# A fused Fourier-mixing and attention kernel: an earlier wait on the last value product, row steps and casts moved between engines, zero rows loaded from DRAM

## The chip, the cores and the metric

The kernel runs on one core of a Trainium2 chip. A core has a matrix engine (TensorE; in the profile PE for its matmuls and PEld for its weight loads), a vector engine (VectorE, DVE), a scalar engine (ScalarE, ACT), a general engine (GpSimd, POOL), and a sync engine (SP) that here issues most DMA transfers. Each engine works through its own list of instructions in order; semaphores make one wait for another. The metric is the device time of one execution, in microseconds (us).

## The reference

Inputs are a sequence x of 2048 rows and 512 columns, two pairs of DFT matrices (2048x2048 and 512x512, real and imaginary), the weights of an attention layer with 32 heads of 16 columns, and a gate vector.

```python
x = A_x
g = sigmoid((x * gate_w).sum(-1, keepdims=True))
a = x @ dft_hid_re.T ;  b = x @ dft_hid_im.T
fourier = dft_seq_re @ a - dft_seq_im @ b
q, k, v = split(x @ wqkv)                     # 32 heads, 16 columns each
p = softmax(q @ k.T * 16 ** -0.5)             # per head, 2048 x 2048
attention = concat(p @ v) @ wo
out = g * fourier + (1 - g) * attention
```

All is in 32-bit floats. The weights of the attention layer are drawn large, so the scores are large, and the maximum of each row has to be subtracted before the exponential.

## The kernel before

**Split operands.** Most matmuls take operands in a fast 32-bit format that keeps fewer bits. A number is therefore split into a rounded part and a rest (a cast and a subtraction, `hi_lo` at line 101 and similar pairs of lines), and a product is the sum of three matmuls.

**Pairs of heads.** The 32 heads are taken as 16 pairs p. For each pair two tiles, `qs` and `ks` (two buffers each, so pairs p and p + 2 share one), hold on 128 partitions two stacks of 64 rows, one for each head h of the pair. Rows 0 to 47 of a stack are the split parts of q and k. Rows 48 and 49 of `ks` are ones, and the same rows of `qs` hold the negated row maximum, again in two parts, so that the score matmul subtracts the maximum by itself. Rows 50 to 63 are zeros. `load_stacks` (line 264) loads a pair's stacks on SP's queue; the ones and zeros are put in at the start (lines 327 to 335), from a small tile that has the tile name `hl` in the profile, and from the third pair on `load_stacks` clears the two maximum rows from a DRAM tensor of zeros, `z_d`.

**Row maxima ahead of scores.** Each score tile (128x512) is computed twice. `a_tile` (line 281) multiplies q by k for a tile and VectorE reduces it to row maxima (`mx`, line 289). When 64 such tiles, half a pair (p, hf), are done, two row steps are put into the list `deferred`. `m_parts` (line 296) takes the maximum over the four tiles of a row, negated (`nm`), and splits it into `nhl`. `m_rows` (line 304) transposes `nhl` into `mt` on VectorE and issues eight DMAs that write it as rows 48 and 49 of `qs`, some on SP's queue, the others on GpSimd's. Later `scores` (line 772) computes the transposed tile with these rows and ScalarE takes its exponential into `pt` (line 786).

**Value products.** A unit u is one block of 128 keys for one half of the queries of a pair; its four exponential tiles lie in `pts[u]`. `pv` (line 813) multiplies them by v, in four column strips of the array at a time, into the accumulator bank `acc` (line 829). A 32-bit matmul runs here as two instructions, so that a unit has eight in the profile. `evacuate` (line 799) copies `acc` on ScalarE (line 806) and GpSimd adds the copy to a running total (line 807). After two segments of half a pair the total is stored.

**Fourier matmuls beside it.** The DFT chains (`real`, `dft`, then `proj` for the output projection; matmuls at line 461) are cut into half-height matmuls of 64 rows. Each runs on one half of the array while a score or maxima matmul, which has 64 rows too, runs on the other. Chunks of the DFT matrices are loaded on SP's queue (`craw`), and `c_split` (line 437) splits them on GpSimd (lines 445 and 446).

**The order is written out by hand.** `segment` (line 936) goes through a pattern of slots. A slot with a letter issues one Fourier matmul and, beside it, a maxima tile (a) or a score tile (s); a digit names its PSUM bank; a bar issues the value products of one unit. There are short phases THIN and NINE at the ends, and in between 192 segments with this pattern:

```python
FULL = "a5 s4 a2 s0 a3 s6 a5 s4 s1 s0 s2 a6 a3 a4 s5 a1 | |"
```

The accumulator shares bank 6 with a6, and it is closed and copied out at each segment's end. The last value product of a FULL segment has an added wait on the last exponential issued (line 951), which is that of s5, in slot 14. At the end of a segment one entry of `deferred` is run, so that `m_parts` stands at the end of one segment and `m_rows` at the end of the next. In the FULL phase the 64th tile of a half pair comes at slot 6.

**Blocks.** Finished heads are normalised in 12 blocks (`block`, line 602): step 0 loads, step 1 multiplies on GpSimd, step 2 splits the result and stores it; here the cast is on ScalarE (line 102) and the subtraction on GpSimd (line 103). `run_plan` runs such steps at fixed units, ahead of a segment.

Of the kernel before, what the change touches and what calls it, by code (L numbers as in the profile page):

```python
# [17 lines left out]
D = 512  # L18
# [13 lines left out]
def mix_kernel(ctx: ExitStack, tc: tile.TileContext, xa_t, xa, wqkv, w_hid, w_seq, wo, gate_w, out):  # L32
# [40 lines left out]


    qk_d = [dram.tile([2, D, S], F32, name=f"qk{c}") for c in range(2)]
    z_d = dram.tile([2, S], F32, name="z")
    b_d = [dram.tile([P, 2, D], F32, name=f"b{s}") for s in range(NT)]
    o_d = [dram.tile([NP, 64, S // 2], F32, name=f"o{hf}") for hf in range(2)]
    yr_d = [dram.tile([P, D], F32, name=f"yr{t}") for t in range(NT)]
# [184 lines left out]
    def load_stacks(p):  # L264
        q_t, k_t = qs[p % 2], ks[p % 2]
        for h in range(2):
            rows = slice((2 * p + h) * DH, (2 * p + h + 1) * DH)
            o = 64 * h
            if p > 1:
                nc.sync.dma_start(q_t[o + 48:o + 50].bitcast(F32), z_d)  # L270

            for i, (qv, kv) in enumerate(((0, 0), (0, 1), (1, 0))):
                part = slice(o + 16 * i, o + 16 * i + 16)
                nc.sync.dma_start(q_t[part].bitcast(F32), qk_d[0][qv, rows])
                nc.sync.dma_start(k_t[part].bitcast(F32), qk_d[1][kv, rows])
# [5 lines left out]
    def a_tile(i, h, ps=None, bank=None):  # L281
        p, j = divmod(i, 64)
        qt, kb = divmod(j, 4)
        if ps is None:
            ps = psA.tile([P, 512], F32, "a", bank)
        r = slice(64 * h, 64 * h + 64)
        nc.tensor.matmul(ps, qs[p % 2][r, qt * P:(qt + 1) * P], ks[p % 2][r, kb * 512:(kb + 1) * 512],  # L287
                         start=True, stop=True)
        user = nc.vector.tensor_reduce(mx[p % 2][:, h, qt, kb:kb + 1], ps, AX.X, ALU.max)  # L289
        hf = j // 32  # L290
        a_left[p, hf] = a_left.get((p, hf), 64) - 1
        if not a_left[p, hf]:
            deferred.extend((partial(m_parts, p, hf), partial(m_rows, p, hf)))
        return user

    def m_parts(p, hf):

        nc.vector.tensor_reduce(nm[hf].rearrange("p (q h) -> p h q", h=2), mx[p % 2][:, :, 8 * hf:8 * hf + 8, :],
                                AX.X, ALU.max, negate=True)
        t = nhl[hf]  # L300
        nc.gpsimd.tensor_copy(t[:, 0], nm[hf])
        nc.gpsimd.tensor_tensor(t[:, 1], nm[hf], t[:, 0].bitcast(F32), ALU.subtract)

    def m_rows(p, hf):

# [21 lines left out]
    for i in range(2):  # L327
        for h in range(2):
            for tb in range(2):
                cols = slice(tb * 2 * D, (tb + 1) * 2 * D)  # L330
                nc.sync.dma_start(ks[i][64 * h + 48:64 * h + 50, cols].bitcast(F32), ones)
                nc.sync.dma_start(ks[i][64 * h + 50:64 * h + 64, cols].bitcast(F32), zeros[:14])
                nc.sync.dma_start(qs[i][64 * h + 48:64 * h + 64, cols].bitcast(F32), zeros)
    for tb in range(2):
        nc.sync.dma_start(z_d[:, tb * 2 * D:(tb + 1) * 2 * D], zeros[:2])
    wrs = []
    a_next = 0

# [263 lines left out]
    def block(step, hf, ct, half):  # L602

        if step == 0:
            t = work.tile([P, 2, D], F32, name="no")
            load_o(t[:, 0], t[:, 1], hf, ct, half * D)
            blocks[hf, ct] = t
        elif step == 1:
            t = blocks[hf, ct]
            nc.gpsimd.tensor_tensor(t[:, 0], t[:, 0], t[:, 1], ALU.mult)  # L610
        else:
            t = blocks.pop((hf, ct))
            hl = work.tile([P, 2, D], F32R, name="nh")
            hi_lo(hl[:, 0], hl[:, 1], t[:, 0], nc.gpsimd)
            nc.sync.dma_start(oh_d[hf][ct][:, :, half * D:(half + 1) * D], hl.bitcast(F32))

    last_o = []
# [154 lines left out]
    def scores(u, qb, h, bank=(psS, "s"), number=None):  # L772
        p, r = divmod(u, 32)
        hf, kt = divmod(r, 16)
        q0 = hf * 1024 + qb * 512
        if u >= UNITS - 16:

            blk, kt = divmod(kt, 8)
            q0, kt = 1024 + blk * 512, 2 * kt + qb
        if u not in pts:  # L780
            pts[u] = work.tile([P, 4, 512], F32, name="pt", bufs=4)
        pool, name = bank
        ps = pool.tile([P, 512], F32, name=name) if number is None else pool.tile([P, 512], F32, name, number)
        rr = slice(64 * h, 64 * h + 64)
        nc.tensor.matmul(ps, ks[p % 2][rr, kt * P:(kt + 1) * P], qs[p % 2][rr, q0:q0 + 512], start=True, stop=True)  # L785
        return nc.scalar.activation(pts[u][:, 2 * qb + h], ps, AF.Exp, bias=0.0, scale=DH ** -0.5)  # L786

# [22 lines left out]
                nc.sync.dma_start(o_d[hf][p, :, qb * 512:(qb + 1) * 512], total[64 * qb:64 * qb + 64])  # L810
            total = None

    def pv(u, full=False, close=False):
        nonlocal acc
        if u >= UNITS - 16:
            return pv_last(u)
        p, r = divmod(u, 32)
        hf, kt = divmod(r, 16)
        pt = pts.pop(u)
        begin, done = acc is None or kt == 0, kt == NT - 1  # L820
        if acc is None:
            acc = psO.tile([P, 512], F32, "acc")
            if not full:
                nc.vector.memset(acc, 0.0)  # L824
        width = 32 if full and begin else 17
        v = vt[:, kt].rearrange("p n d -> p (n d)")[:, 33 * p:]
        for j in range(4):
            h = j % 2
            i = nc.tensor.matmul(acc[32 * j:32 * j + width], v[:, 16 * h:16 * h + width], pt[:, j],  # L829
                                 start=begin, stop=done or close)  # L830
# [86 lines left out]
    thin = 1 + 4 * (NT - 3)  # L917
    streams = [stream(h) for h in range(2)]

    users, valued, exponential = [], 0, None  # L920

    def score(kind, h, number=None):
        nonlocal exponential
        x = next(streams[h][kind == "a"], None)
        if x:
            users.append((kind, a_tile(*x, bank=number) if kind == "a" else scores(*x, number=number)))
            if kind == "s":
                exponential = users[-1][1]

    def values(full=False, close=False):  # L930
        nonlocal valued
        i = pv(valued, full, close)
        valued += 1
        return i

    def segment(pattern, half, ds, stop):
# [4 lines left out]
        ds, turned = iter(ds), False  # L941
        for n, slot in enumerate(pattern.split()):
            number = None
            if slot[1:].isdigit():
                slot, number = slot[0], int(slot[1])
            if slot == "|":
                end = n == len(pattern.split()) - 1
                i = values(pattern == FULL, end and (pattern == FULL or valued == thin))
                if end and pattern == FULL:

                    tc.add_manual_dep(i.ins, exponential.ins.name,
                                      mybir.DependencyInfo(mybir.DependencyClass.Sync, mybir.DependencyReason.DATA))
                while between:
                    between.pop(0)()
# [123 lines left out]
```

## Time and profile before

| | us |
|---|---|
| three runs | 1697.93, 1702.73, 1703.36 |
| their median | 1702.73 |
| the profiled execution, device time | 1700.88 |
| its span, first to last instruction | 1699.1 |
| TensorE busy in the span | 1683.4 |
| VectorE busy | 1371.5 |
| ScalarE busy | 1250.0 |
| GpSimd busy | 661.6 |
| mean granted TensorE clock | 0.997 |

How to read it: the page and the views give times from the span's start. A group row has line, engine, operation, tiles (out<-in), shapes, count, then busy us and mean ns of one, then the idle time of the engine ahead of the group and what ended most of it. A row of waits is: who waited, for what, us in total, times, the longest. A row of the timeline is: start, duration, engine, line, operation, with neighbours of one group merged and their count after x. TensorE's busy time overlaps its own pipelining, so 99% does not say that nothing can be gained there; the idle and the length of a stage say more.

### The profile page before, as it was taken

To read this page: it belongs to the slowest core of one execution; us is meant where nothing else is said; L and a number is where in the kernel's file an instruction comes from. 1 tells how busy PE (TensorE), PEld (TensorE's weight loads), DVE (VectorE), ACT (ScalarE), POOL (GpSimd) and SP (SyncE) were. 2 spreads that over 40 slices of the span, in tenths; PEclk is the share of its full clock that TensorE was granted. 3 is DMA by queue.
4 is the path that set the end of the run, shared out by engine and by line. 5 is a ranking of instruction groups with operands and counts; after the bars stand their busy time and mean duration, and the time that the engine had idled before them with its cause. 6 is when DMAs were issued, how large, how long until landed. Compare 5 with 4: busy or idle time off the path is not lost.

```text
span 1699.1 us, 34567 instructions
## 1 busy us (share of the span) xinstructions
PE 1683.4 (99%) x13040; PEld 1024.1 (60%) x13040; DVE 1371.5 (81%) x2290; ACT 1250.0 (74%) x2435; POOL 661.6 (39%) x724
## 2 busy tenths in 40 slices
PE   9999999999999999999999999999999999999998
PEld 7878855556665656666565555556656556645444
DVE  5429888888888888888888888888888788889954
ACT  5212377787887888788877788878888788878886
POOL 0202112333544556444444465554444555421110
PEclk9999999999999999999999999999999999999999
DMA  9963600314241433314157434324142535452114
GB/s 290 349 141 132 184 10 2 58 33 82 57 77 46 85 101 94 77 39 83 38 95 249 97 102 108 76 60 73 52 83 70 118 99 103 141 169 46 35 32 138
DMA packets 82882, 166.63 MB, mean 98 GB/s; under 512 B 19760, under 2 KB 20254, under 8 KB 78818
## 3 DMA queue, kind: packets, MB, share of 16 engines
q1 hardware_dynamic: 78474, 163.45, 38.0%
q8 instruction: 103, 1.69, 0.5%
q0 software_dynamic: 3808, 0.30, 0.2%
q14 instruction: 65, 0.53, 0.1%
q10 hardware_dynamic: 432, 0.66, 0.1%
HBM read 108.19 MB, written 54.53 MB: 96 GB/s over the span
## 4 chain that ended last, share of the span: by engine, by line
PE 95%; DMA 3%; POOL 1%; issue 0%; SPq 0%; DVE 0%; ACT 0%; DVEq 0%; POOLq 0%
PE acc L829 28%; PE d L461 25%; PE a L287 17%; PE s L785 15%; PE s L375 3%; PE d L375 1%; PE acc L793 1%; DMA ks<-qk 1%; PE a L108 1%; PE a L106 1%; PE s L108 1%; PE s L106 1%; PE a L107 1%; PE s L107 1%; DMA raw<-wo 1%; PE s L461 1%
## 5 line engine op out<-in xcount | busy, mean ns | idle before, releaser
L289 DVE TENSOR_REDUCE mx<-a 128x1 f32<-128x512 f32 x2026 | 1258.8, 684 | 220.3 <-PE a L287 186.7
L786 ACT ACTIVATE pt<-s 128x512 f32<-128x512 f32 x2006 | 1022.6, 623 | 78.2 <-PE s L785 60.2
L287 PE MATMUL a<-ks,qs 64*128 64x512 f32 x2026 | 729.8, 405 | 2.5 <-DMA qs<-hl 2.5
L785 PE MATMUL s<-qs,ks 64*128 64x512 f32 x2006 | 692.8, 402 | 3.7 <-ACT few L806 2.7
L461 PE MATMUL d<-xab,ch 64*128 64x512 f32 x2016 | 646.3, 395 | 0.0
L829 PE MATMUL acc<-pt,vt 128*17 128x512 f32 (+1 forms) x3968 | 502.1, 600 | 2.0 <-DVE acc L824 2.0
L287 PEld LDWEIGHTS a<-ks,qs 64*128 64x128 f32 x2026 | 367.5, 184 | 224.5 <-issue 165.5
L807 POOL TENSOR_TENSOR oe<-oe,few 128x512 f32<-128x512 f32 x169 | 218.4, 1293 | 489.8 <-ACT few L806 481.4
L785 PEld LDWEIGHTS s<-qs,ks 64*128 64x128 f32 x2006 | 363.1, 184 | 65.3 <-issue 18.4
L461 PE MATMUL d<-xab,cl 64*128 64x512 f32 x1008 | 398.3, 395 | 0.0
L461 PEld LDWEIGHTS d<-xab,ch 64*128 64x128 f32 x2016 | 365.5, 184 | 29.3
L806 ACT COPY few<-acc 128x512 f32<-128x512 f32 x169 | 99.1, 586 | 189.4 <-PE acc L829 178.2
L829 PEld LDWEIGHTS acc<-pt,vt 128*17 128x17 f32 (+1 forms) x3968 | 103.6, 101 | 217.6 <-issue 155.7
L461 PEld LDWEIGHTS d<-xab,cl 64*128 64x128 f32 x1008 | 185.6, 184 | 15.1
L446 POOL TENSOR_TENSOR cl<-craw,ch 128x512 fp32r<-128x512 f32 x126 | 162.0, 1286 | 10.2
L445 POOL CAST ch<-craw 128x512 fp32r<-128x512 f32 x126 | 77.2, 613 | 52.9 <-PE s L785 31.6
L461 PE MATMUL d<-wre,xab 64*128 64x512 f32 x336 | 90.4, 402 | 0.0
L461 PEld LDWEIGHTS d<-wre,xab 64*128 64x128 f32 x336 | 58.8, 184 | 38.7 <-issue 23.3
L312 POOL DMA_DIRECT2D qs<-mt x119 | 67.0, 568 | 27.2 <-DVE mx L289 10.0
L461 PE MATMUL d<-wo_hl,o_hl 64*128 64x512 f32 (+1 forms) x246 | 68.1, 409 | 0.0
L461 PEld LDWEIGHTS d<-wo_hl,o_hl 64*128 64x128 f32 (+1 forms) x246 | 42.3, 184 | 29.8 <-issue 12.2
L102 ACT CAST hl<-s 128x512 fp32r<-128x512 f32 x28 | 16.1, 588 | 58.3 <-PE s L375 23.6
(171 smaller groups left out, 1044.1 us busy)
## 6 DMA issues: line engine op xcount, KB each, us to landing
craw<-w_seq SPq DMA_DIRECT2D x128, 256.0 KB
qk<-hl SPq DMA_DIRECT2D x32, 512.0 KB
qs<-qk SPq DMA_DIRECT2D x96, 128.0 KB
ks<-qk SPq DMA_DIRECT2D x96, 128.0 KB
b<-hl SPq DMA_DIRECT2D x16, 512.0 KB
xab<-b SPq DMA_DIRECT2D x16, 512.0 KB
o<-oe SPq DMA_DIRECT2D x62, 128.0 KB
oh<-nh SPq DMA_DIRECT2D x12, 512.0 KB
```

What stands on the lines that cost most here:

```text
L287: nc.tensor.matmul(ps, qs[p % 2][r, qt * P:(qt + 1) * P], ks[p % 2][r, kb * 512:(kb + 1) * 512], start=True, stop=True)
L289: user = nc.vector.tensor_reduce(mx[p % 2][:, h, qt, kb:kb + 1], ps, AX.X, ALU.max)
L312: (nc.gpsimd if own else nc.sync).dma_start(rows.rearrange("v (q b c) -> v b q c", q=8, b=4)[:, b], mt[hf][32 * b + h:32 * b + 32:2])
L375: i = nc.tensor.matmul(ps, st[r], mv[r], start=not half and not j, stop=half == 1 and j == 11)
L445: nc.gpsimd.tensor_copy(h1, raw)
L446: nc.gpsimd.tensor_tensor(l1, raw, h1.bitcast(F32), ALU.subtract)
L461: i = nc.tensor.matmul(self.ps, st[r], mv[r], start=not self.begun, stop=stop)
L785: nc.tensor.matmul(ps, ks[p % 2][rr, kt * P:(kt + 1) * P], qs[p % 2][rr, q0:q0 + 512], start=True, stop=True)
L786: return nc.scalar.activation(pts[u][:, 2 * qb + h], ps, AF.Exp, bias=0.0, scale=DH ** -0.5)
L806: nc.scalar.copy(few, acc)
L807: nc.gpsimd.tensor_tensor(total, total, few, ALU.add)
L829: i = nc.tensor.matmul(acc[32 * j:32 * j + width], v[:, 16 * h:16 * h + width], pt[:, j], start=begin, stop=done or close)
```

## The change

- The last value product of a FULL segment waits for the second-last exponential issued (slot s2) in place of the last (slot s5).
- In a FULL segment one entry of `deferred` is also run ahead of slot 8, so that a row step can stand in the middle of a segment.
- The split of the negated maxima in `m_parts` moves from GpSimd to VectorE.
- The cast of a block's split moves from ScalarE to GpSimd.
- The zeros of rows 48 to 63 are no longer loaded at the start. `z_d` grows to 16 rows, and `load_stacks` loads the zero rows of pairs 1 and 2 from it (from pair 3 on the two maximum rows alone, as before). For pair 0 the maxima matmuls read 48 rows and the score matmuls 50.
- A freshly opened accumulator is always written 32 columns wide by its first product, and the memset for the other case (line 824) goes.

```diff
-    z_d = dram.tile([2, S], F32, name="z")
+    z_d = dram.tile([16, S], F32, name="z")
...
-            if p > 1:
-                nc.sync.dma_start(q_t[o + 48:o + 50].bitcast(F32), z_d)
+            if p:
+                n = 64 if p < 3 else 50
+                nc.sync.dma_start(q_t[o + 48:o + n].bitcast(F32), z_d[:n - 48])
+                if p < 3:
+                    nc.sync.dma_start(k_t[o + 50:o + 64].bitcast(F32), z_d[:14])
...
-        r = slice(64 * h, 64 * h + 64)
+        r = slice(64 * h, 64 * h + (64 if p else 48))
...
-        nc.gpsimd.tensor_copy(t[:, 0], nm[hf])
-        nc.gpsimd.tensor_tensor(t[:, 1], nm[hf], t[:, 0].bitcast(F32), ALU.subtract)
+        nc.vector.tensor_copy(t[:, 0], nm[hf])
+        nc.vector.tensor_tensor(t[:, 1], nm[hf], t[:, 0].bitcast(F32), ALU.subtract)
...
-                cols = slice(tb * 2 * D, (tb + 1) * 2 * D)
-                nc.sync.dma_start(ks[i][64 * h + 48:64 * h + 50, cols].bitcast(F32), ones)
-                nc.sync.dma_start(ks[i][64 * h + 50:64 * h + 64, cols].bitcast(F32), zeros[:14])
-                nc.sync.dma_start(qs[i][64 * h + 48:64 * h + 64, cols].bitcast(F32), zeros)
+                nc.sync.dma_start(ks[i][64 * h + 48:64 * h + 50, tb * 2 * D:(tb + 1) * 2 * D].bitcast(F32), ones)
     for tb in range(2):
-        nc.sync.dma_start(z_d[:, tb * 2 * D:(tb + 1) * 2 * D], zeros[:2])
+        nc.sync.dma_start(z_d[:, tb * 2 * D:(tb + 1) * 2 * D], zeros)
...
-            hi_lo(hl[:, 0], hl[:, 1], t[:, 0], nc.gpsimd)
+            nc.gpsimd.tensor_copy(hl[:, 0], t[:, 0])
+            nc.gpsimd.tensor_tensor(hl[:, 1], t[:, 0], hl[:, 0].bitcast(F32), ALU.subtract)
...
-        rr = slice(64 * h, 64 * h + 64)
+        rr = slice(64 * h, 64 * h + (64 if p else 50))
...
-    def pv(u, full=False, close=False):
+    def pv(u, close=False):
...
-        begin, done = acc is None or kt == 0, kt == NT - 1
+        begin, done, width = acc is None or kt == 0, kt == NT - 1, 17
         if acc is None:
             acc = psO.tile([P, 512], F32, "acc")
-            if not full:
-                nc.vector.memset(acc, 0.0)
-        width = 32 if full and begin else 17
+            width = 32
...
-                exponential = users[-1][1]
+                exponentials.append(users[-1][1])
...
+            if n == 8 and pattern == FULL and deferred:
+                deferred.pop(0)()
...
-                    tc.add_manual_dep(i.ins, exponential.ins.name,
+                    tc.add_manual_dep(i.ins, exponentials[-2].ins.name,
```

More of the change, by code (lines that the diff above doesn't have):

```diff
@@ L918, in mix_kernel @@
     streams = [stream(h) for h in range(2)]
-    users, valued, exponential = [], 0, None
+    users, valued, exponentials = [], 0, []
     def score(kind, h, number=None):
-        nonlocal exponential
         x = next(streams[h][kind == "a"], None)
@@ L927, in score, with values @@
             if kind == "s":
-                exponential = users[-1][1]
-    def values(full=False, close=False):
+                exponentials.append(users[-1][1])
+    def values(close=False):
         nonlocal valued
-        i = pv(valued, full, close)
+        i = pv(valued, close)
         valued += 1
@@ L947, in segment @@
                 end = n == len(pattern.split()) - 1
-                i = values(pattern == FULL, end and (pattern == FULL or valued == thin))
+                i = values(end and (pattern == FULL or valued == thin))
                 if end and pattern == FULL:
-                    tc.add_manual_dep(i.ins, exponential.ins.name,
+                    tc.add_manual_dep(i.ins, exponentials[-2].ins.name,
                                       mybir.DependencyInfo(mybir.DependencyClass.Sync, mybir.DependencyReason.DATA))
```

## The prediction

> **What bounds the kernel now.** First the page: span, busy times and the chain that ended last.
>
> ```profile
> span 1699.1 us, 34567 instructions
> PE 1683.4 (99%) x13040; PEld 1024.1 (60%) x13040; DVE 1371.5 (81%) x2290; ACT 1250.0 (74%) x2435; POOL 661.6 (39%) x724
> PE 95%; DMA 3%; POOL 1%; issue 0%; SPq 0%; DVE 0%; ACT 0%; DVEq 0%; POOLq 0%
> ```
>
> TensorE (PE) sets the pace, so an edit is worth what it takes out of PE's own time. Next the table by stretches over the 192 FULL segments, all instructions first, then the value products alone (line 829).
>
> ```profile
> 363.50:1488.60 1125.10, 1121.37 (x9188) 674.23 (x9188) 959.63 (x1586) 905.00 (x1767) 558.11 (x601) 1.00 0.38 88
> 363.50:1488.60 1125.10, 384.08 (x3072) 88.30 (x3072) 1.00 0.38 88
> ```
>
> Columns: length, then busy time and count of PE, weight loads, VectorE, ScalarE, GpSimd, clock, DMA. A segment takes 1125.1/192 = 5.86 us, of which the products of two units take 384.08/192 = 2.00. Now one segment in the timeline (start, duration); its sixteen matmul pairs run from 803.94 to about 807.8, its value products from 807.82.
>
> ```profile
> 804.47 5.04 DVE L289 TENSOR_REDUCE mx<-a 128x1 f32<-128x512 f32 x8 [0.77 <-PE a L287]
> 807.82 0.16 PEld L829 LDWEIGHTS acc<-pt,vt 128*32 128x32 f32 x8 [0.31 <-DVE mx L289]
> 808.07 0.67 ACT L786 ACTIVATE pt<-s 128x512 f32<-128x512 f32 x1
> 808.79 0.11 PEld L829 LDWEIGHTS acc<-pt,vt 128*17 128x17 f32 x2
> 809.76 0.18 PEld L287 LDWEIGHTS a<-ks,qs 64*128 64x128 f32 x1 [0.85 <-issue]
> ...
> 902.56 1.92 PE L829 MATMUL acc<-pt,vt 128*32 128x512 f32 x16
> ```
>
> The last exponential ends at 808.74; the two last weight loads start at 808.79, right behind it: the added wait binds. In the segment at 902.56, where PE had come late and the exponentials were done in time, the same sixteen products take 1.92.
>
> **The change part by part.**
>
> *The wait moved to the second-last exponential.* Gain per segment 2.00 - 1.92 = 0.08 us; over 192 segments 15 us, and 14 if 1.92 stands for 1.927. I take 14.7. The second-last exponential ends some half microsecond earlier (next part's row: 8 in about 4 us), before the last product needs it. What is late next: the first maxima matmul of the next segment uses the bank that the last exponential reads, so the wait moves to it; it starts at 809.76, one microsecond after 808.74. ScalarE's next piece, the copy of the accumulator, waits for PE anyhow. Bounds 0 (if another wait takes its place) and 15.4.
>
> *Block casts from ScalarE to GpSimd, 12 of them.* First product loads of four segments around one such cast, and the cast:
>
> ```profile
> 590.77 0.16 PEld L829 LDWEIGHTS acc<-pt,vt 128*32 128x32 f32 x8 [0.35 <-DVE mx L289]
> 596.88 0.16 PEld L829 LDWEIGHTS acc<-pt,vt 128*32 128x32 f32 x8 [0.24 <-DVE mx L289]
> 602.79 0.16 PEld L829 LDWEIGHTS acc<-pt,vt 128*32 128x32 f32 x8 [0.33 <-DVE mx L289]
> 608.61 0.16 PEld L829 LDWEIGHTS acc<-pt,vt 128*32 128x32 f32 x8 [0.30 <-DVE mx L289]
> ...
> 593.33 0.62 ACT L102 CAST nh<-no 128x512 fp32r<-128x512 f32 x1
> ...
> L102 ACT CAST nh<-no 128x512 fp32r<-128x512 f32 x12 | 7.5, 623 | 0.0
> L445 POOL CAST ch<-craw 128x512 fp32r<-128x512 f32 x126 | 77.2, 613 | 52.9 <-PE s L785 31.6
> L807 POOL TENSOR_TENSOR oe<-oe,few 128x512 f32<-128x512 f32 x169 | 218.4, 1293 | 489.8 <-ACT few L806 481.4
> ```
>
> The cast delays all eight exponentials behind it: the segment takes 6.11 against 5.82. That is 0.29 x 12 = 3.5 us; the longer wait in the products (5.91 after it) is already in the 14.7. On GpSimd a cast of this size takes 613 ns, 12 of them 7.4 us. They lie in its 490 us of idle time before the accumulator's additions. Where that cover is gone (GpSimd late because a chunk arrived late) ScalarE's copy waits for it: twice at most, 1.2 us. The store behind it on SP's queue leaves 0.6 later, far ahead of its reader. I take 3.5, ends 2.3 and 3.5.
>
> *Zero rows.* Sixteen loads of zeros go from SP's queue in the start; the first matmuls read 48 rows and do not wait for them. Ahead of pair 1 four loads of 14 or 16 rows are added on that queue, ahead of pair 2 two, and two more grow from 2 to 16 rows; the zeros written to DRAM grow from 2 to 16 rows. They are issued when the pair before begins, and the first matmul that needs them comes some 30 us later or more: cost 0, and if one were late, no more than the 2.5 us below.
>
> ```profile
> L287 PE MATMUL a<-ks,qs 64*128 64x512 f32 x2026 | 729.8, 405 | 2.5 <-DMA qs<-hl 2.5
> 121.40:124.80 3.40, 3.28 (x16) 2.85 (x18) 0.69 (x1) 0.00 (x0) 0.00 (x0) 0.50 0.47 75
> ...
> L829 PE MATMUL acc<-pt,vt 128*17 128x512 f32 x2432 | 332.6, 597 | 2.0 <-DVE acc L824 2.0
> 1493.50:1497.00 3.50, 3.50 (x18) 0.99 (x14) 1.75 (x3) 1.57 (x3) 0.00 (x0) 0.51 1.06 423
> ...
> 1350.00:1358.00 8.00, 5.87 (x48) 3.02 (x46) 4.37 (x8) 4.44 (x9) 7.43 (x7) 1.00 0.51 175
> PEld s L785 <- ACT few L806: 2.6, 1, 2.6
> ```
>
> The load of zeros (its source bears the name hl) held PE for 2.5 us, and from 121.4 to 124.8 the granted clock was 0.50: half of 3.4 us more. Gain 2.5 + 1.7 = 4.2.
>
> *The memset that goes.* The one at line 824 stands in VectorE's queue behind eight reductions and held the first product after the FULL segments for 2.0 us; the clock was then 0.51 for 3.5 us. With 32 columns written by the first product nothing is to be cleared. Gain 2.0 + 1.7 = 3.7. The half clock is tied to the two stalls by its place alone: a stall of 2.6 us near 1352 left it at 1.00. So both gains lie between the stalls alone (4.5) and 7.9.
>
> The Trainium skill, "TensorE: Matmul & The Clock Gate", Part 1, says that the clock halves after an idle window of about 3.4 us. Here 2.5 and 2.0 us of idling stand ahead of it, less than that window; by that rule these stalls are not its cause, and the sum would be 3.4 us higher.
>
> *Row steps earlier, row split on VectorE.* After four of eight score tiles in the FULL segment that ends a half pair, VectorE now does the maximum, a cast and a subtraction; the transpose and its eight DMAs (four from SP, four from GpSimd at 0.57 each) come at the same segment's end, one segment earlier. They stand then in SP's queue behind this segment's chunk loads, and on GpSimd behind the addition, where the next segment brings no chunk. The rows land about 6 us sooner. Gain: the one wait for them,
>
> ```profile
> PE s L785 <- DMA qs<-mt: 1.0, 1, 1.0
> PEld s L785 <- issue: 1.4, 1, 1.4
> ```
>
> the second row being the same stall at the weight load: 1.4 us, once. The price is on VectorE.
>
> ```profile
> PEld acc L829 <- DVE mx L289: 61.0, 192, 0.4
> L298 DVE TENSOR_REDUCE nm<-mx 128x16 f32<-128x64 f32 x24 | 5.0, 209 | 0.0
> L766 DVE TENSOR_SCALAR ng<-g x1: 175/175/175, 199.4 to 199.4; 128x16 f32<-128x16 f32 x1
> 836.17 2.48 DVE L289 TENSOR_REDUCE mx<-a 128x1 f32<-128x512 f32 x4
> 838.57 0.21 DVE L298 TENSOR_REDUCE nm<-mx 128x16 f32<-128x64 f32 x1
> 839.43 0.69 DVE L289 TENSOR_REDUCE mx<-a 128x1 f32<-128x512 f32 x1 [0.65 <-PE a L287]
> 835.14 0.61 POOL L445 CAST ch<-craw 128x512 fp32r<-128x512 f32 x1
> 835.84 1.29 POOL L446 TENSOR_TENSOR cl<-craw,ch 128x512 fp32r<-128x512 f32 x1
> L620 DVE CAST o_lno<-o_raw x1: 417/417/417, 1639.4 to 1639.4; 128x512 fp32r<-128x512 f32 x1
> ```
>
> At the end of a segment the maximum (838.57) was covered by 0.65 us in which VectorE waits for PE. In the middle it stands ahead of the fifth reduction, which frees the bank that the value products write: the first row says that their first load waits for this reduction in every segment. The work is 0.21 + 2 x 0.17 (a small VectorE operation of 128x16) = 0.55 us. Against it stands slack: eight reductions in 5.04 are six steps of 0.60 and one of 0.75, so 0.15 idle before the fifth, and some 0.1 more between its end and the load. I take 0.32 per step, 24 steps (the count in the second row): 7.7 us, with ends of 5 (more slack) and 13 (none).
>
> The sum: -14.7 - 3.5 - 4.2 - 3.7 - 1.4 + 7.7 = -19.8 against the profiled execution's 1700.9, so 1681. That execution is 1.85 below the median of the three runs; against the median the forecast is 1683.
>
> **The rivals.**
>
> *VectorE's split waits for GpSimd.* At the new place GpSimd is at work in each of the 24 segments: at 836.2 it had begun the subtraction of 835.84, which lasts to 837.13. No row shows a VectorE operation with two operands in SBUF, or a fast cast (417 ns for 512 columns: two per cycle of the 684 ns reduction's pace) beside one of GpSimd, so the trace is silent on whether they hold each other. If the cast must wait until 837.1, the fifth reduction comes 1.2 us late; where GpSimd's cast is running, its subtraction follows and the split's own subtraction waits for that too, some 1.9. With 1.4 on average 24 steps cost 34 instead of 7.7: 1709, slower. It decides from 1.15 per step (27.5 gained elsewhere, over 24). If only the subtraction waits, some 0.8 each, it is 1695. For it: the operands and the time fall together. Against: the reduction of 838.57's kind ran beside GpSimd elsewhere at the same 209 ns.
>
> The Trainium skill, "SBUF — State Buffer", section Who interferes with whom, says that a VectorE cast in the two-port mode, or one of its operations with two SBUF inputs, and a GpSimd operation share a port pair under an exclusive lock: the second blocks until the first is done, and a reduction never does. By that rule this rival is what happens, with 1709.
>
> *The wait only moves.* The next segment's first matmul, or a bank further on, waits as long: 1683 + 14.7 = 1698, no clear change. Against it: the 1.0 us between 808.74 and 809.76.
>
> *48 and 50 rows break the pairing* of the two halves of the array. All row-split matmuls shown have 64 or 32 rows. 256 matmuls of pair 0 would each take a slot of 0.23 of their own: +58, 1741. For it only that no such form is shown.
>
> **How the numbers follow.** Forecast 1683: 0.48, own range 1677 to 1692 (row steps 5 to 13, the half clocks, the wait term). Split held by GpSimd: 0.27 in full, 0.10 half. Wait moves: 0.09. Pairing broken: 0.03; the rest is open. 0.3% (5 us) is about what a measurement tells from no change: faster 0.62, same 0.14, slower 0.24. The range takes in the lock rival: 1675 to 1713.
>
> **What the profile of the changed kernel would show.** The last two loads of a segment's products a few hundredths behind the others, and 1.92 to 1.93 us of products; no 6.1 us segment at the blocks; no wait on hl near 120 and none on acc at the first product after FULL, and no half clock at either place; the step's cast and subtraction on VectorE at 0.1 to 0.2 each and the products of that segment 0.3 late. A cast or subtraction of 0.5 to 1.4 us there, or a gap ahead of it, is the first rival. Products at 2.0 still, or a new wait on the last exponential, is the second. The forecast also fails if the late chunks that held PE near 976 and 1352 grow, since GpSimd has more to do there.

## The result: 0.2% slower, and the profile after

The changed kernel takes 1702.62 us (median of 20 runs, 1701.37 to 1704.44); the kernel before took 1699.06 in the 20 runs beside it (1696.28 to 1703.36). The ratio is 1.0019, with a 95% interval of 1.0012 to 1.0026: by it 3.2 us slower, within the 0.3% that I called no change. I had forecast a gain of 19.8 us. (The median of three runs that the forecast set out from, 1702.73, lay 3.7 above the one of twenty.) Of the twelve runs of the kernel with the block casts alone, reported below, one took 3251.5 us; it counts in the median given there but not in the ratio.

The page of the changed kernel, with the span and the chain that ended last by engine and by line:

```profile
span 1700.5 us, 34533 instructions
PE 90%; DVE 7%; DMA 2%; issue 0%; POOL 0%; SPq 0%; ACT 0%; DVEq 0%; POOLq 0%
PE acc L828 27%; PE d L461 21%; PE a L290 16%; PE s L786 14%; DVE mx L292 5%; PE s L375 3%; PE s L407 1%; DVE nhl L304 1%; PE acc L794 1%; PE d L375 1%; DMA ks<-qk 1%; DMA craw<-w_seq 1%; PE s L108 1%; PE a L108 1%; PE a L107 1%; PE s L107 
```

Before, VectorE (DVE) had 0% of that chain. Now it has 7%: the reductions, and the cast of the row split, line 304, which did not stand on VectorE before. (In the changed kernel the value products are line 828, the maxima reductions 292, the split 304 and 305. The numbers shift by a few lines from kernel to kernel; the tile names stay.)

The table by stretches of the changed kernel: the FULL phase, its value products alone, and the two places where the clock had been halved. Columns: length, busy time and count of PE, weight loads, then (where there are five) VectorE, ScalarE, GpSimd; then clock, DMA share, GB/s.

```profile
363.50:1490.60 1127.10, 1102.28 (x9174) 664.82 (x9176) 980.21 (x1631) 895.60 (x1751) 555.77 (x564) 1.00 0.37 87
...
363.50:1490.60 1127.10, 367.60 (x3060) 75.96 (x3064) 1.00 0.37 87
...
121.40:124.80 3.40, 3.40 (x34) 2.77 (x32) 2.75 (x5) 0.00 (x0) 0.00 (x0) 1.00 0.30 107
1493.50:1497.00 3.50, 3.50 (x30) 1.65 (x30) 3.02 (x6) 2.42 (x6) 1.08 (x1) 1.00 0.98 377
```

The products became shorter as forecast: 367.60/3060 is 0.1201 each, 1.92 per segment of sixteen, against 384.08/3072, 2.00. That is 15.0 us over 192 segments. Both stretches of half clock are gone. Yet the FULL phase is not shorter: from the first product load of its first segment to that of its last it took 1122.9 before and 1126.9 now. So PE is busy 19 us less in FULL (1102.28 against 1121.37) and idle 21 us more (24.8 of the stretch against 3.7). What it waits for, the table of waits says (us in total, times, longest):

```profile
PEld acc L828 <- DVE mx L292: 84.8, 192, 1.8
PE acc L828 <- DVE mx L292: 21.7, 24, 1.4
```

Before, the first of these rows had 61.0 us and never more than 0.4 at a time. The second row did not exist, and its count is that of the row steps in FULL. (The two describe the same idle time, once at the weight load and once at the matmul.) The groups of VectorE within FULL:

```profile
L304 DVE CAST nhl<-nm 128x16 fp32r<-128x16 f32 x24 | 16.0, 665 | 0.8
L305 DVE TENSOR_TENSOR nhl<-nm,nhl 128x16 fp32r<-128x16 f32 x24 | 6.3, 261 | 0.8
L301 DVE TENSOR_REDUCE nm<-mx 128x16 f32<-128x64 f32 x24 | 5.3, 220 | 0.8
```

I had put 0.17 each on the cast and the subtraction. They took 0.665 and 0.261 on average. Two of the 24 steps in the timeline (start, duration), the first at 651, the second at 839, with GpSimd (POOL) beside them:

```profile
651.11 0.61 POOL L445 CAST ch<-craw 128x512 fp32r<-128x512 f32 x1 [0.70 <-PE d L461]
651.54 0.21 DVE L304 CAST nhl<-nm 128x16 fp32r<-128x16 f32 x1
651.79 0.18 DVE L305 TENSOR_TENSOR nhl<-nm,nhl 128x16 fp32r<-128x16 f32 x1
...
838.74 1.28 POOL L446 TENSOR_TENSOR cl<-craw,ch 128x512 fp32r<-128x512 f32 x1
838.99 0.22 DVE L301 TENSOR_REDUCE nm<-mx 128x16 f32<-128x64 f32 x1
839.24 0.82 DVE L304 CAST nhl<-nm 128x16 fp32r<-128x16 f32 x1
840.09 0.17 DVE L305 TENSOR_TENSOR nhl<-nm,nhl 128x16 fp32r<-128x16 f32 x1
840.18 2.48 DVE L292 TENSOR_REDUCE mx<-a 128x1 f32<-128x512 f32 x4
840.92 0.16 PEld L828 LDWEIGHTS acc<-pt,vt 128*32 128x32 f32 x8 [1.42 <-DVE mx L292]
```

At 839 GpSimd has begun its subtraction when the cast is issued. The cast ends at 840.06, just behind GpSimd's end at 840.02; the reduction ahead of it, also beside GpSimd, took its normal 0.22. The fifth reduction starts 1.2 us after the maximum did, and PE's next load waits 1.42 instead of some 0.33. At 651 VectorE's cast comes when GpSimd's cast has only 0.18 us left (it ends at 651.72), and takes 0.21. Of the 24 steps, 18 have a cast of 0.77 to 0.84 us and 6 one of 0.18 to 0.23.

The same thing stands in THIN, where I had not looked for it, since a step at a segment's end seemed covered:

```profile
231.54 1.30 POOL L480 TENSOR_TENSOR xab<-y,xab 128x512 fp32r<-128x512 f32 x1
232.12 0.75 DVE L304 CAST nhl<-nm 128x16 fp32r<-128x16 f32 x1
233.73 0.18 PEld L290 LDWEIGHTS a<-ks,qs 64*128 64x128 f32 x1 [0.78 <-DVE mx L292]
```

This occurs at 232, 279 and 325. My theory from these rows: VectorE's split waits for GpSimd (the first rival of the prediction), and the four other edits do what I said. The rival to it: the steps cost what VectorE has to do there, and the rest of the loss lies elsewhere.

### The profile page after: what moved, and what is told of

Its sections match the earlier page's. It is cut to its first block, busy times and chain, and to the rows that moved or that the text cites. A ratio compares the mean times of both kernels' runs of the same rounds, so it can differ in the third digit from the quotient of the medians.

```text
span 1700.5 us, 34533 instructions
## 1 busy us (share of the span) xinstructions
PE 1666.7 (98%) x13040; PEld 1014.8 (60%) x13040; DVE 1397.7 (82%) x2353; ACT 1242.7 (73%) x2423; POOL 656.9 (39%) x672
## 4 chain that ended last, share of the span: by engine, by line
PE 90%; DVE 7%; DMA 2%; issue 0%; POOL 0%; SPq 0%; ACT 0%; DVEq 0%; POOLq 0%
PE acc L828 27%; PE d L461 21%; PE a L290 16%; PE s L786 14%; DVE mx L292 5%; PE s L375 3%; PE s L407 1%; DVE nhl L304 1%; PE acc L794 1%; PE d L375 1%; DMA ks<-qk 1%; DMA craw<-w_seq 1%; PE s L108 1%; PE a L108 1%; PE a L107 1%; PE s L107 1%
## 5 line engine op out<-in xcount | busy, mean ns | idle before, releaser
L290 PE MATMUL a<-ks,qs 64*128 64x512 f32 (+1 forms) x2026 | 726.3, 404 | 1.1 <-DVE mx L292 1.1
L786 PE MATMUL s<-qs,ks 64*128 64x512 f32 (+1 forms) x2006 | 690.8, 401 | 3.1 <-ACT few L807 3.1
L828 PE MATMUL acc<-pt,vt 128*17 128x512 f32 (+1 forms) x3968 | 486.6, 598 | 21.7 <-DVE mx L292 21.7
L290 PEld LDWEIGHTS a<-ks,qs 64*128 64x128 f32 (+1 forms) x2026 | 366.4, 184 | 221.3 <-issue 139.8
L786 PEld LDWEIGHTS s<-qs,ks 64*128 64x128 f32 (+1 forms) x2006 | 365.1, 185 | 65.2 <-issue 16.8
L828 PEld LDWEIGHTS acc<-pt,vt 128*17 128x17 f32 (+1 forms) x3968 | 91.6, 101 | 236.7 <-issue 151.6
L479 POOL CAST xab<-y 128x512 fp32r<-128x512 f32 x16 | 9.8, 611 | 138.9 <-ACT y L477 95.4
```

## The experiments: what a row step costs

Each ratio is against runs of the kernel before in the same session; the medians of those were 1701.0 for the first four kernels of this section, 1700.1 for its last three and the row part alone, and 1699.3 for the others. A difference of about 1 us between two kernels of different sessions therefore says little by itself.

**Three reductions in place of the split.** The mid-segment step does the maximum and two dummy reductions; the cast and the subtraction follow at the segment's end.

```diff
-        nc.vector.tensor_copy(t[:, 0], nm[hf])
-        nc.vector.tensor_tensor(t[:, 1], nm[hf], t[:, 0].bitcast(F32), ALU.subtract)
+        if middle:
+            for i in range(2):
+                nc.vector.tensor_reduce(spare_nm[i].rearrange("p (q h) -> p h q", h=2),
+                                        mx[p % 2][:, :, 8 * hf:8 * hf + 8, :], AX.X, ALU.max, negate=True)
+            unsplit.append(hf)
+        else:
+            split(hf)
...
     def m_rows(p, hf):
+        while unsplit:
+            split(unsplit.pop())
```

> Changed kernel with, at the mid-segment place, three reductions of 128x64 (0.22 us each, two of them dummies) in place of the reduction, cast and subtraction (0.22 + 0.17 + 0.17 unheld); the cast and the subtraction stand at the segment's end, ahead of the transpose. VectorE's own work ahead of the fifth reduction is thus kept (0.66 against 0.57 us), and only operations that GpSimd held in the trace (cast 0.82, subtraction 0.52) are gone from there. Hold theory (VectorE's split waits for GpSimd): the 24 steps cost 24 x 0.4 = 10 instead of about 25 us, so about 1687. Work theory (the steps cost what VectorE has to do there): no faster than the changed kernel, 1702 or a little more.

Measured: 1691.59 us, ratio 0.9950 (0.9936 to 0.9964). Faster by 11 us than the changed kernel, as the hold would have it, and 4.6 above the 1687 of that theory (four splits at a segment's end are held here, as in the next run, and those segments take 6.52 to 6.55). But the equal work that I promised was not equal, as VectorE's timeline of this run shows:

```profile
833.46 0.22 DVE L303 TENSOR_REDUCE nm<-mx 128x16 f32<-128x64 f32 x1
833.59 0.34 DVE L308 TENSOR_REDUCE nms<-mx 128x16 f32<-128x64 f32 x2
833.85 2.47 DVE L294 TENSOR_REDUCE mx<-a 128x1 f32<-128x512 f32 x4
```

Reductions that do not depend on each other start 0.13 apart, though each takes 0.22, so three cost 0.39. The unheld split costs 651.88 - 651.29 = 0.6 from the maximum to the next reduction, since each of its steps reads the one before. The run shows that reductions are not held (GpSimd's subtraction ran from 833.22 to 834.52 beside them), but not yet how the price divides. That is worked out below (the run with four dummy reductions).

**Row steps at segment ends only.**

```diff
-            if n == 8 and pattern == FULL and deferred:
-                deferred.pop(0)()
```

> Changed kernel without the run of a row step ahead of slot 8; the steps stand at segment ends as before, with the split still on VectorE. Hold theory: at the segment's end GpSimd has finished its chunk and VectorE has some 0.65 us of cover, so the 24 steps cost 0 to 2; the row wait of 1.4 comes back; the three THIN steps stay held (3 us): 1678 to 1682. Work theory as I forecast it (7.7 us for 24 steps, the rest of the loss elsewhere): 1694 to 1697.

Measured: 1686.01 us, ratio 0.9924 (0.9905 to 0.9943): 17 less than the changed kernel, 4 to 8 above what I expected. Most of that is in its trace: where an addition of the DFT output (y, yr) runs on GpSimd at the segment's end, the split is held there too, four times, and its cover does not suffice:

```profile
1021.49 1.04 DVE L304 CAST nhl<-nm 128x16 fp32r<-128x16 f32 x1
1022.57 0.52 DVE L305 TENSOR_TENSOR nhl<-nm,nhl 128x16 fp32r<-128x16 f32 x1
...
1021.22 1.29 POOL L520 TENSOR_TENSOR y<-y,yr 128x512 f32<-128x512 f32 x1 [1.35 <-ACT y L519]
1022.45 0.61 POOL L445 CAST ch<-craw 128x512 fp32r<-128x512 f32 x1
```

The cast waits for one GpSimd operation and the subtraction for the next. These four segments take 6.56 to 6.60 us, against 5.75 for the others: 3.3 us together, beside the three steps in THIN. PE's wait for the rows, too, is 2.4 us here, against 1.0 in the kernel before. In sixteen of the 24 steps GpSimd is idle when the cast comes, and the same cast takes 0.17.

**The split back on GpSimd, step still ahead of slot 8.**

```diff
-        nc.vector.tensor_copy(t[:, 0], nm[hf])
-        nc.vector.tensor_tensor(t[:, 1], nm[hf], t[:, 0].bitcast(F32), ALU.subtract)
+        nc.gpsimd.tensor_copy(t[:, 0], nm[hf])
+        nc.gpsimd.tensor_tensor(t[:, 1], nm[hf], t[:, 0].bitcast(F32), ALU.subtract)
```

> Changed kernel with the split back on GpSimd, row steps still mid-segment. Hold theory: only the 0.22 us reduction stands ahead of the fifth reduction, within 0.15 of slack, so 24 steps cost 2 to 4, and the three steps in THIN are no longer held (3 us won): 1675 to 1681. Work theory: 0.35 x 24 = 8 us won, 1694.

Measured: 1677.41 us, ratio 0.9870 (0.9851 to 0.9890). One line pair moved back gives 25 us and a kernel 1.3% faster than before. No segment of FULL is above 6 us any more but for three at or right behind late chunks (below). In the phases before FULL, from the 600th to the 2400th matmul, it takes 229.9 us where the changed kernel takes 233.1: 3.2 in THIN. From the last FULL segment to the end it takes 208.7 against 210.0: 1.3 there, where one of the four casts is held (0.57).

**The step ahead of slot 12**, behind the reduction of a6, whose bank the products write.

```diff
-            if n == 8 and pattern == FULL and deferred:
+            if n == 12 and pattern == FULL and deferred:
```

> Changed kernel with the mid-segment row step ahead of slot 12 instead of slot 8, thus behind the reduction of a6, the one whose bank the value products write. If the loss comes through that bank alone, the steps cost 0 to 4 whether VectorE is held or not: 1679 to 1684. If a held VectorE is late for whatever reads its maxima next (the three reductions behind, then the next segment's first banks), it costs again 10 us or more: 1690 to 1700.

Measured: 1690.55 us, ratio 0.9949 (0.9932 to 0.9966), so the second of the two. The wait moves to the next segment's Fourier matmuls (d), which now stand behind the late reductions:

```profile
PEld d L461 <- DVE mx L292: 8.6, 16, 1.0
PE d L461 <- DVE mx L292: 4.0, 6, 0.7
```

Neither row exists in the changed kernel. The place decides who waits; the hold is there at either place (six casts of 0.89 to 0.93 us). It is rarer here, though: seventeen of the 24 casts come when GpSimd's operation is nearly done and take 0.17 to 0.23. So the 12 us gained over the changed kernel are not the worth of the place alone.

**The row part without late chunks.** Of three further kernels the base is the last one of the next section, with the split on GpSimd and later stack loads (1669.97 us). First with the split on VectorE:

> The kernel with later stack loads (1670.0), split back on VectorE, so that the row part stands alone without late chunks. Hold theory with the sizes of the trace: 24 x 0.96 in FULL, 3.2 in THIN, 1.3 behind FULL: 27.5 more, 1697. My sum's 0.32 per step: 7.7 more, 1678.

Measured: 1697.28 us, ratio 0.9982 (0.9972 to 0.9991): 27.3 more than the base. Its wait for the reductions, and then the base's:

```profile
PEld acc L828 <- DVE mx L292: 85.0, 192, 1.8
```

```profile
PEld acc L828 <- DVE mx L292: 62.2, 192, 0.4
```

85.0 - 62.2 = 22.8, or 0.95 per step. With the 3.2 in THIN and the 1.3 behind FULL that is 27.3: the whole of the loss.

Then with the split on GpSimd and four dummy reductions behind the maximum, work that is not held:

```diff
+        for i in range(4 if middle else 0):
+            nc.vector.tensor_reduce(spare_nm[i].rearrange("p (q h) -> p h q", h=2),
+                                    mx[p % 2][:, :, 8 * hf:8 * hf + 8, :], AX.X, ALU.max, negate=True)
         nc.gpsimd.tensor_copy(t[:, 0], nm[hf])
```

> The kernel with later stack loads and the split on GpSimd (1670.0), and at the mid-segment place four dummy reductions of 128x64 behind the maximum: they start 0.13 apart, so VectorE gets about 0.65 us of work ahead of the fifth reduction, as with the unheld cast and subtraction, and nothing that GpSimd held. Work as in the few unheld steps of the changed kernel (0.48 us each): 11.5 more, 1681 to 1682, which leaves the other half of the steps' price to the hold. If the work alone were the price: 23 more, 1693. By my 0.32: 1678.

Measured: 1681.99 us, ratio 0.9893 (0.9878 to 0.9908): 12.0 more than the base. Its timeline and its wait for the reductions:

```profile
830.29 0.22 DVE L303 TENSOR_REDUCE nm<-mx 128x16 f32<-128x64 f32 x1
830.43 0.58 DVE L307 TENSOR_REDUCE nms<-mx 128x16 f32<-128x64 f32 x4
830.93 2.47 DVE L294 TENSOR_REDUCE mx<-a 128x1 f32<-128x512 f32 x4
...
830.04 1.29 POOL L451 TENSOR_TENSOR cl<-craw,ch 128x512 fp32r<-128x512 f32 x1
```

```profile
PEld acc L833 <- DVE mx L294: 74.1, 192, 0.9
```

The fifth reduction starts 0.64 after the maximum (830.93 - 830.29), about as with the unheld split, with GpSimd at work all the while and no operation longer for it. 74.1 - 62.2 = 11.9, or 0.50 per step. So of the 0.95 about a half is VectorE's work and a half is the hold. The changed kernel says the same within itself: its six segments with an unheld step take 6.22 to 6.26, that is 0.48 above the usual 5.76; twelve with the cast held take 6.80 to 6.86, mostly 1.09 above; four with the subtraction held as well take 7.19 or 7.20, 1.43 above; the last two meet late chunks.

And the base without the mid-segment step (as in the run with row steps at segment ends only, here with the split on GpSimd):

> The kernel with later stack loads and the split on GpSimd (1670.0), without the row step ahead of slot 8: steps at segment ends as before. If the rows' earlier landing is worth its one wait: 1.4 more, 1671 to 1672. If the maximum in the middle costs as much as it saves: 1670.

Measured: 1671.89 us, ratio 0.9837 (0.9822 to 0.9852): 1.9 more than the base, whose list has no such row as this one:

```profile
PE s L786 <- DMA qs<-mt: 2.0, 1, 2.0
```

So the earlier rows are worth their one wait, 1.9 against the 1.4 forecast; the two kernels ran in different sessions, but in their traces FULL differs by as much (1101.3 us against 1099.6). The maximum alone in the middle costs about 1 us over the 24 steps (62.2 against 61.2 in the waits for the reductions).

## The experiments: the other parts one by one

Each of these is the kernel before with one part of the change.

**The wait on the second-last exponential alone.**

```diff
-                    tc.add_manual_dep(i.ins, exponential.ins.name,
+                    tc.add_manual_dep(i.ins, exponentials[-2].ins.name,
```

> The kernel before with one edit: the last value product waits for the second-last exponential. My sum says 14.7 us less than before (192 x 0.076): about 1685. Rival (the wait only moves): no change, 1700; then the gap ahead of the next segment's first maxima matmul would grow by 0.08.

Measured: 1687.73 us, ratio 0.9932 (0.9918 to 0.9946): 11.6 less (9.2 to 13.9). No wait took its place: FULL, measured as above, is 1109.1 us long against 1122.9, 13.7 less. The run also tells something of the clock. Both of the stalls that I had tied to a halved clock are there, and so is the table by stretches right behind each:

```profile
PE a L287 <- DMA qs<-hl: 2.1, 1, 2.1
PE acc L829 <- DVE acc L824: 2.0, 1, 2.0
```

```profile
122.20:125.60 3.40, 3.40 (x32) 3.37 (x32) 2.07 (x4) 0.00 (x0) 0.00 (x0) 1.00 0.39 65
...
1478.00:1481.50 3.50, 3.50 (x30) 1.33 (x24) 2.03 (x4) 1.96 (x4) 0.00 (x0) 1.00 1.07 418
```

The clock stayed at 1.00 after both; the last section says what differs.

**Zero rows and memset alone** (the edits to `z_d`, `load_stacks`, the 48 and 50 rows, and the first product's 32 columns).

```diff
-            if not full:
-                nc.vector.memset(acc, 0.0)
-        width = 32 if full and begin else 17
+        width = 32 if opened else 17
```

> The kernel before with the zero rows from DRAM and the memset gone (the freshly opened accumulator written 32 columns wide). If the half clock hangs on the two stalls: 4.2 + 3.7 = 7.9 us less, 1691 to 1693. If only the stalls go: 4.5 less, 1695 to 1696. If 48 and 50 rows broke the pairing of the halves: 50 us more.

Measured: 1695.26 us, ratio 0.9977 (0.9968 to 0.9986): 3.9 less (2.4 to 5.4). Both stalls are gone from its trace, and the pairing of the halves is unhurt. The size is near that of the stalls alone, but the traces show that more goes into it. Of the two profiled executions this one is shorter by 4.3 us ahead of FULL and by 3.9 behind it, stalls and half clocks both, as I had summed them. The half clocks, however, do not come with every such stall (the run above has the stalls and neither half clock), and FULL is 1.3 longer here, where the wait for the rows has grown from 1.0 us to

```profile
PE s L786 <- DMA qs<-mt: 2.7, 1, 2.7
```

In the three kernels with the zeros loaded at the start and the row steps at segment ends this wait is 0.8 to 1.1 us, in the three such kernels with the zero rows from DRAM 2.0 to 2.7. I had put the cost of the zero rows at 0. Why they lengthen that wait, which comes near 890 us, stays open; in the changed kernel the earlier row step does away with it.

**Block casts on GpSimd alone.**

```diff
-            hi_lo(hl[:, 0], hl[:, 1], t[:, 0], nc.gpsimd)
+            nc.gpsimd.tensor_copy(hl[:, 0], t[:, 0])
+            nc.gpsimd.tensor_tensor(hl[:, 1], t[:, 0], hl[:, 0].bitcast(F32), ALU.subtract)
```

> The kernel before with the block's cast on GpSimd. My sum: 3.5 us less (12 segments of 6.11 become 5.83), 1696 to 1697, or 2.3 less if GpSimd's longer work delays ScalarE's copy where a chunk comes late. Rival: GpSimd's extra 0.6 us meets the late chunks and nothing is won: 1700.

Measured: 1696.05 us, ratio 0.9979 (0.9969 to 0.9989): 3.6 less (1.9 to 5.3). None of its FULL segments takes 6.1 us any more.

**The row part alone**: split on VectorE, step ahead of slot 8.

> The kernel before with the row part alone: split on VectorE, row step ahead of slot 8. From the changed kernel against the one with the split on GpSimd: 25 us more than before, 1722 to 1727, if this part's price does not hang on the others. My sum said 6.3 more (7.7 less the row wait of 1.4): 1706. If the earlier wait of the last product makes the row step dearer (the products' bank then ends the chain alone), less than 20 more here.

Measured: 1721.62 us, ratio 1.0129 (1.0114 to 1.0144): 21.9 more (19.4 to 24.5). This is 3 less than the 25 that separate the changed kernel from the one with its split on GpSimd. Intervals of 2.5 us to each side here, and some 3 there, do not establish that difference. The traces account for some of it: a segment with the cast alone held takes about 6.85 us in both kernels, while the usual one takes 5.83 here and 5.76 there, so that such a step costs 0.07 less here. That is the direction of the last case of the expectation, though not its size. The rest stays open.

**Later stack loads.** The faster the kernel got, the longer it stood at two places. In the run with the split on GpSimd the segments at 958 and 1331 take 10.2 and 10.95 us. The timeline of SP's queue ahead of the first of them:

```profile
940.59 0.59 SPq L596 DMA_DIRECT2D no<-o  x1
...
943.16 0.44 SPq L271 DMA_DIRECT2D qs<-z  x1
943.65 0.33 SPq L277 DMA_DIRECT2D qs<-qk  x1
...
952.36 0.30 SPq L278 DMA_DIRECT2D ks<-qk  x1
953.44 0.36 SPq L435 DMA_DIRECT2D craw<-w_seq  x1
```

The chunk load (`craw`) is issued behind a block's loads and fourteen loads of the next pair's stacks, from 943.2 on. GpSimd's next chunk cast comes at 960.37, after 8.22 us of idling; ScalarE's copy of the accumulator waits for GpSimd, and PE for ScalarE. So the stack loads go two segments later:

```diff
-        at(32 * (p - 1), load_stacks, p)
+        at(32 * (p - 1) + (4 if p > 1 else 0), load_stacks, p)
```

> The changed kernel with the row split on GpSimd (1677.4 when run so) and each pair's stack loads issued two segments later from the second pair on. In the trace of that kernel the two long segments at 958 and 1331 (10.2 and 10.95 instead of 5.76, 9.7 us together) come when a chunk load stands on SP's queue behind a block's loads and twelve stack loads. If that queue is the cause, the two shrink to 7 or less and the time is 1669 to 1674; if the block's loads alone make the chunk late, nothing changes, 1677; if the stacks then come too late for the first maxima of the pair, it is slower than that.

Measured: 1669.97 us, ratio 0.9827 (0.9814 to 0.9839), the fastest here: 1.7% below the kernel before, 1.9% below the changed one. The same place in its queue:

```profile
943.36 0.58 SPq L435 DMA_DIRECT2D craw<-w_seq  x1
```

The chunk is issued 10 us earlier, and not one of the 192 segments takes over 6.0 us. The stacks still come in time.

## Why the prediction was wrong, point by point

| part | forecast, us | measured alone, us |
|---|---|---|
| wait on the second-last exponential | -14.7 | -11.6 (-13.9 to -9.2) |
| zero rows and memset | -4.2 - 3.7 = -7.9 | -3.9 (-5.4 to -2.4) |
| block casts | -3.5 | -3.6 (-5.3 to -1.9) |
| row steps and their split | +7.7 - 1.4 = +6.3 | +21.9 (19.4 to 24.5) |
| sum | -19.8 | +2.8 |
| the changed kernel | -19.8 | +3.2 (2.0 to 4.4) |

The four parts measured alone add up to the whole within intervals of some 2 us each. That the agreement is so close, and that gains and loss cancel to 0.2%, is chance: beside the other parts and with later stack loads the row part costs 25.4 us (1697.28 against 1671.89) and not 21.9, and the zero rows lengthen a wait that the row part then removes. The step that failed is the last term, "I take 0.32 per step, 24 steps: 7.7 us". It measured 0.95 per step, 22.8 us, and another 4.5 outside FULL.

- **Its work was too small.** Slack of 0.25 was taken off 0.55 of work (which leaves 0.30; I took 0.32). Unheld, the work takes 0.60 from the maximum to the next reduction, and 0.48 of it reaches PE (0.64 and 0.50 with the dummy reductions). The slack that counts is some 0.13, not 0.25. That gives 12 for the 24 steps, within the ends of 5 and 13 that I kept, and would have left the forecast faster.
- **The first rival was the mechanism.** It put 1.4 on each step; measured were 0.95 with the work, of which the hold proper is 0.45, as six of the 24 casts come at the end of a GpSimd operation and are hardly held, and a held cast waits only for what is left of it. By itself 0.95 lies below the 1.15 from which, by my sum, it decides; it took the 4.5 us outside FULL and smaller gains elsewhere as well to use up what the other parts won. The row that I held against it, a reduction at its usual 209 ns beside GpSimd, speaks of a form that is not held (the run with dummy reductions). It was no evidence on the cast, and the chance of 0.37 for this rival, full and half together, was too low for a hold that operands and time both pointed to.
- **I counted 24 steps; the split moves in 32.** Three held ones in THIN and the four behind FULL cost 3.2 + 1.3 = 4.5 us. At a segment's end I had costed the step at nothing, with 0.65 of idling as cover; a held cast of 0.75 is not covered.
- **The half clocks were not to be had in every run.** The profiled execution had both, worth the 1.7 us each that I gave them. Of the three further kernels with the same two stalls, one has one half clock there in its trace (the row part alone) and two have none (the wait alone, the block casts alone), so that the full 3.4 us was the upper end. "Tied by its place alone" was the weak point, and I took that end all the same. The part measured 3.9 and not 7.9, and 1.3 of what is missing is FULL with its longer wait for the rows. The Trainium skill's idle window ("TensorE: Matmul & The Clock Gate", Part 1), by which the sum was to be 3.4 us higher, came nearer in size: 4.5 for both against 3.9 measured, which is luck, as the half clock did follow these stalls. As a rule for when the clock halves it did not hold here, as the last section shows.
- **Right:** the last product's wait in its mechanism, 1.92 for the products and no wait in its place; in time it gave 11.6, 3 below the estimate, whose 14.7 lies just outside the interval. The block casts. The one wait for the rows (1.9 for 1.4). The second and third rivals did not occur. The late chunks did take more in the faster kernels, as the prediction's last sentence feared, though not in the changed one, which was not faster.

## What to carry to other kernels

Before moving a small cast or a two-input subtraction to VectorE, look at what GpSimd is doing at that moment: beside a GpSimd operation of 1.29 us an operation of 0.17 us may take up to 1.04, and its place in VectorE's queue decides who pays. A reduction beside GpSimd is evidence only for reductions. Where an edit sits in a helper, count every call of it, not only those in the phase under study; and when the bound engine gets faster, look again at loads that share a queue with the ones that feed it.

## What the runs showed of the hardware

**The hold.** VectorE's cast of 128x16 ended some 30 ns after the GpSimd operation that was running when it was issued, whether that was GpSimd's cast (0.61 us) or its subtraction or addition (1.29), and its subtraction of two SBUF operands did so as well (0.52 where it met GpSimd's cast). Reductions kept their length. This agrees with the Trainium skill, "SBUF — State Buffer", section Who interferes with whom, which says that a cast in the two-port mode and an operation with two SBUF inputs on VectorE block against a GpSimd operation for its whole length, and a reduction does not. The prediction gave that rule too small a chance.

**The half clock.** In the profiled execution of the kernel before, PE's waits of 2.5 and 2.0 us were followed by half clock and one of 2.6 was not. With the last product's wait alone changed, waits of 2.1 and 2.0 at the same two places were not. The traces show what tells them apart. Within an execution the stretches at half clock begin a whole number of 3.413 us apart (before: at 121.37 and 1493.53, which is 402 times 3.4133) and last 3.41 us, in one case 6.83. The three waits of the kernel before, cut into windows on that grid (length, then busy time of PE and weight loads, VectorE, ScalarE, GpSimd, then the clock):

```profile
117.96:121.37 3.41, 1.07 (x9) 0.56 (x5) 0.69 (x1) 0.00 (x0) 0.00 (x0) 1.00 0.25 42
121.37:124.78 3.41, 3.26 (x16) 2.83 (x18) 0.69 (x1) 0.00 (x0) 0.00 (x0) 0.50 0.46 75
1350.17:1353.58 3.41, 1.89 (x15) 1.04 (x11) 1.89 (x3) 0.02 (x1) 3.17 (x4) 1.00 0.14 48
1353.58:1356.99 3.41, 2.79 (x21) 1.68 (x21) 1.47 (x3) 3.41 (x8) 3.33 (x4) 1.00 0.72 261
1490.12:1493.53 3.41, 1.43 (x14) 0.53 (x10) 2.42 (x5) 1.12 (x3) 0.46 (x1) 1.00 1.02 375
1493.53:1496.94 3.41, 3.41 (x18) 0.99 (x14) 1.69 (x3) 1.57 (x3) 0.00 (x0) 0.50 1.06 423
```

Where PE was busy for 1.07 or 1.43 of the 3.41 us, the clock of the next window was halved; where a window's edge cut the wait in two and 1.89 were left, it was not. In all 14 traces, the last 10 us of each left out, PE is busy for 1.03 to 1.62 us of the window ahead of each of the seven half clocks, and for 1.75 or more of every other window. So 2 us of idling halved the clock when they fell into one window, and a gap of 2.7 us cut into 1.2 and 1.5 (zero rows alone, at 895) did not. This is read from one execution of each kernel, with ends of matmuls that the profile models. The grid stands differently against the work in each trace: at the first stall an edge lies at 121.37 in the kernel before and at 119.76 in the one with the block casts alone. If it shifts between executions of one kernel as well, which is not shown, that would account for a part of the spread: over 22 runs of the kernel before, the mean granted clock went from 0.997 to 1.000, and the time with it, 1700.6 on average at 0.997 and 1697.7 at 0.999. The Trainium skill ("TensorE: Matmul & The Clock Gate", Part 1) has an idle window of about 3.4 us. The length is that of the grid here, but gaps shorter than the window were enough, and the measurement decides.

**Small reductions overlap.** Independent reductions of 128x64 took 0.21 to 0.22 us each but started 0.13 apart.
